# Attention with its backward pass: Q and dO turned by the crossbar, next head's loads gated, usual path last, last turns early

## The chip, the cores and the metric

One core of one Trainium2 chip. The metric is the device time of one execution in microseconds (us). Every comparison is with the kernel before, run on the same chip in the same rounds.

## The reference, cut to what matters

The forward function is a layer norm, attention of 32 heads (2048 queries, 2048 keys, head size 128, width 576), and a gated feed-forward block; the output is `x + s * g`. What is computed is the output and the gradients of nine arguments.

```python
def _A_ref(x, k_cache, v_cache, wq, wo):
    q = (x @ wq).reshape(B, Sq, H, Dh).transpose(0, 2, 1, 3)
    p = softmax(einsum("bhqd,bhkd->bhqk", q, k_cache) * Dh ** -0.5)
    o = einsum("bhqk,bhkd->bhqd", p, v_cache)
    return o.transpose(0, 2, 1, 3).reshape(B, Sq, H * Dh) @ wo
...
_out, _vjp = jax.vjp(_f, A_x, A_k_cache, A_v_cache, A_wq, A_wo, ...)
return (_out, *_vjp(grad_out))
```

## The kernel before

Attention takes 3053 of 4944 us. A head has two phases of 16 query tiles. In the first, TensorE makes the scores of a tile, ScalarE their exponentials (the tile Pq), and SyncE has the crossbar turn Pq into PT (128 x 2048, 0.52 MB), which TensorE needs six tiles later for `o`. In the second, dP is made, VectorE forms dS in the place of Pq, SyncE has it turned into dST, and TensorE needs that six tiles later for `dq`. The row sums' inverse `rinv` is not put into P but into dOn and Qn, the natural layouts of dO and Q, on VectorE. QT and KT, the turned Q and K, are two halves of one tile KQ, and the profile calls both KQ: `Qn<-KQ` is Q turned back, `KQ<-Kn` is K turned.

```python
def transpose_slab(hs, qt, name):            # PT and dST, 32 a head, all on SyncE
    T = wpt.tile([P, NT, P], bf, name=name, tag="PT")      # 8 buffers
    nc.sync.dma_start_transpose(T[:], hs.slabs[qt][:])
def turn_nat(dst, src): nc.sync.dma_start_transpose(...)   # VT, KT: one each a head
def prep_don(hs, sc): pe_transpose_blocks(... dOT -> dOn)  # TensorE, then a copy by VectorE
def prep_qn(hs):      pe_transpose_blocks(... QT -> Qn)    # TensorE, then a copy by VectorE
def scale_qn(hs, qt): nc.vector.tensor_scalar(Qn[:, qt], Qn[:, qt], rinv[:, qt], op0=mult)
def tail1(hs, qt, part):                     # o = P V, and junk = -(o . dOn), into negdelta
    tail_part(hs, hs.PT[qt], hs.Vn, part) ...
# ... the plan of a head: b1, b2 = first slot of its two phases, pl = second phase of the head before
for c in range(4):
    put(pl + q(c), 0, lambda c=c: load_k(hd(), c, 4))            # 4 pieces of 128 KB
    put(pl + q(skew + 3 + c), 0, lambda c=c: load_v(hd(), c, 4))
put(pl + q(4), 0, lambda: load_wo(hd()))
put(pl + q(5), 0, lambda: load_wq(hd()))
```

`put` names a slot of the program, but the scheduler that orders each engine's instructions moves them; a place is only sure if a dependency holds it. Loads and stores are issued by GpSimd, turns by SyncE, each strictly in order.

## Time and profile before

| | us |
|---|---|
| median of 3 runs (lowest to highest) | 4947.64 (4942.96 to 4948.25) |
| span of the profiled run | 4943.5 |
| attention, first score matmul to the first matmul after it | 3052.8 |
| one steady head (mean of 28 heads, from PT 0 to the next PT 0) | 95.0 |

### The profile page before, as it was taken

The page shows a single profiled execution, that of the slowest core. Times are in us where ns is not written, and L with a number is a line of the kernel's source. Part 1 is how long each engine was busy: PE and PEld are TensorE (multiplying, and loading weights), DVE is VectorE, ACT ScalarE, POOL GpSimd, SP SyncE. Part 2 cuts the span into 40 slices and gives each one's busy share as a digit, 9 for nine tenths or more (in the row PEclk, how much of TensorE's full clock was granted, in tenths as well). Part 3 has the DMA queues.
Part 4 walks back from the last instruction along what each step waited for, and adds up shares of the span by engine and source line. Part 5 has one row for each costly group of instructions (what it writes and reads, how often), then busy time and mean ns, then how long its engine had stood idle before and what let it go on. Part 6 is the DMA issues. An engine that isn't in the chain of part 4 may idle for free. (4 is left out here: it accounts for less than half of the span.)

```text
span 4943.5 us, 101621 instructions
## 1 busy us (share of the span) xinstructions
PE 4877.6 (99%) x41029; PEld 2892.8 (59%) x41029; DVE 2802.9 (57%) x6554; ACT 2473.9 (50%) x4228; POOL 843.4 (17%) x1329
## 2 busy tenths in 40 slices
PE   9999999999999999999999999999899999999998
PEld 4445666666666666666666666666455555555554
DVE  4544666666566666666656666666434555554225
ACT  4431766766676676676666667667312111111011
POOL 3322111111111111111111111111221111111111
PEclk9999999999999999999999999999999999999999
DMA  7887999999999999999999999999999999998665
GB/s 260 274 202 173 225 222 225 228 229 230 222 231 224 230 225 237 219 227 220 235 220 231 233 224 229 231 221 231 210 225 235 223 234 218 233 226 204 195 168 151
DMA packets 3048181, 1097.68 MB, mean 222 GB/s; under 512 B 2951890, under 2 KB 2956115, under 8 KB 3047699
## 3 DMA queue, kind: packets, MB, share of 16 engines
q1 hardware_dynamic: 2948930, 771.66, 83.4%
q0 software_dynamic: 98160, 318.85, 20.3%
q8 instruction: 322, 5.28, 0.4%
q14 instruction: 161, 1.31, 0.1%
q10 hardware_dynamic: 608, 0.59, 0.0%
HBM read 175.31 MB, written 177.93 MB: 71 GB/s over the span
## 5 line engine op out<-in xcount | busy, mean ns | idle before, releaser
L654 ACT ACTIVATE Pq<-sp 128x1024 bf16<-128x1024 f32 x1024 | 1048.0, 1024 | 268.7 <-PE sp L636 259.4
L709 DVE SCALAR_TENSOR_TENSOR Pq<-dp,negdelta,Pq 128x1024 bf16<-128x1024 f32 x512 | 655.2, 1280 | 44.5 <-PE dp L706 44.5
L712 ACT ACTIVATE t<-dp,negdelta 128x1024 bf16<-128x1024 f32 x512 | 567.6, 1115 | 214.3 <-PE dp L706 199.8
L636 PE MATMUL sp<-KQ 128*128 128x512 bf16 x2048 | 609.6, 379 | 2.2 <-ACT Pq L654 2.1
L706 PE MATMUL dp<-VT,dOT 128*128 128x512 bf16 x2048 | 609.2, 379 | 2.3
L683 PEld LDWEIGHTS <-dST 128*128 128x128 bf16 x8192 | 506.8, 98 | 155.5 <-DMA dST<-Pq 16.3
L683 PEld LDWEIGHTS <-PT 128*128 128x128 bf16 x8192 | 499.8, 98 | 133.6 <-DMA PT<-Pq 14.1
L683 PE MATMUL acc<-Kn,dST 128*128 128x128 bf16 x8192 | 556.3, 219 | 9.0 <-DMA dST<-Pq 8.8
L683 PE MATMUL acc<-Vn,PT 128*128 128x128 bf16 x8192 | 542.0, 219 | 8.6 <-DMA PT<-Pq 8.3
L713 DVE TENSOR_TENSOR Pq<-t,Pq 128x1024 bf16<-128x1024 bf16 x512 | 354.6, 693 | 319.3 <-ACT t L712 307.0
L744 PE MATMUL acc<-Pq,dOn 128*128 128x512 bf16 x2048 | 531.1, 379 | 0.0
L744 PE MATMUL acc<-Pq,Qn 128*128 128x512 bf16 x2048 | 526.7, 380 | 0.0
L724 ACT ACTIVATE dq_n<-acc,rsc 128x128 bf16<-128x128 f32 x512 | 187.7, 367 | 335.1 <-PE acc L683 313.6
L1154 DVE TENSOR_TENSOR dxn<-acc,dxn 128x576 f32<-128x576 f32 x272 | 206.1, 758 | 248.1 <-PE acc L1054 248.1
L744 PEld LDWEIGHTS <-Qn 128*128 128x128 bf16 x2048 | 200.4, 98 | 240.8 <-issue 1.5
L744 PEld LDWEIGHTS <-dOn 128*128 128x128 bf16 x2048 | 198.9, 98 | 233.8
L1116 ACT ACTIVATE ndh<-dh 128x512 bf16<-128x512 f32 x144 | 86.0, 597 | 452.5 <-DVE du_blk L1114 448.7
L641 DVE TENSOR_REDUCE rs_all<-rsp 128x1 f32<-128x2 f32 x512 | 78.4, 153 | 306.4 <-ACT Pq L654 294.8
L636 PEld LDWEIGHTS <-KQ 128*128 128x128 bf16 x2048 | 179.3, 98 | 124.4 <-issue 4.0
L706 PEld LDWEIGHTS <-dOT 128*128 128x128 bf16 x2048 | 178.7, 98 | 124.6 <-issue 12.4
L677 POOL DMA_DIRECT2D on_d<-o_n x128 | 97.4, 761 | 784.3 <-DVE junk L695 460.3
L677 POOL DMA_DIRECT2D dq_d<-dq_n x128 | 98.2, 768 | 721.4 <-ACT dq_n L724 681.7
(208 smaller groups left out, 6827.6 us busy)
## 6 DMA issues: line engine op xcount, KB each, us to landing
out_dram<-kvn POOLq DMA_DIRECT2D x64, 512.0 KB, 4.8
ah<-a_d POOLq DMA_DIRECT2D x18, 1024.0 KB, 9.3
ah<-h_d POOLq DMA_DIRECT2D x18, 1024.0 KB, 11.7
h_d<-h_row POOLq DMA_DIRECT2D x64, 256.0 KB, 3.5
a_d<-a_row POOLq DMA_DIRECT2D x64, 256.0 KB, 3.9
x_all<-in_A_k_cache_dram SPq DMA_DIRECT2D x64, 256.0 KB, 4.0
on_d<-o_n POOLq DMA_DIRECT2D x128, 128.0 KB, 4.6
kvT_d<-KQ POOLq DMA_DIRECT2D x32, 512.0 KB, 5.7
```

The source lines that it names most:

```text
L636: nc.tensor.matmul(sp[:, c * CH:(c + 1) * CH], lhsT=hs.QT[:, qt * P:(qt + 1) * P], rhs=hs.KT[:, hf * HW_ + c * CH: hf * HW_ + (c + 1) * CH ...
L654: nc.scalar.activation(Pq[:, hsl], sp[:], AF.Exp, scale=SCALE, accum_out=hs.rsp[:, hf:hf + 1])
L677: nc.gpsimd.dma_start(dst_d[q0 * P:(qt + 1) * P, hs.h * P:(hs.h + 1) * P].rearrange("(t p) d -> p t d", p=P), buf[:])
L683: nc.tensor.matmul(hs.acc[:, 0, :], lhsT=T[:, kt, :], rhs=rhs[:, kt, :], start=(kt == 0), stop=(kt == NT - 1))
L706: nc.tensor.matmul(dp[:, c * CH:(c + 1) * CH], lhsT=hs.dOT[:, qt * P:(qt + 1) * P], rhs=hs.VT[:, hf * HW_ + c * CH: hf * HW_ + (c + 1) * C ...
L709: nc.vector.scalar_tensor_tensor(Pq[:, hsl], dp[:], hs.negdelta[:, qt:qt + 1], Pq[:, hsl], op0=ALU.add, op1=ALU.mult)
L712: nc.scalar.activation(t[:], dp[:], AF.Identity, bias=hs.negdelta[:, qt:qt + 1], scale=1.0)
L713: nc.vector.tensor_tensor(Pq[:, hsl], t[:], Pq[:, hsl], op=ALU.mult)
L724: nc.scalar.activation(hs.dq_n[:, qt % G4, :], hs.acc[:, 0, :], AF.Copy, scale=hs.rsc[:, qt:qt + 1])
L744: nc.tensor.matmul(self.acc, lhsT=self.nat[:, qt, :], rhs=self.slabs[qt][:, cs], start=(qt == self.lo), stop=(qt == self.hi - 1))
L1116: nc.scalar.mul(ndh[:], dh[:], -1.0)
L1154: nc.vector.tensor_tensor(dxn[:, st, :], acc[:, :D], dxn[:, st, :], op=ALU.add)
```

## The change

The intent: take 1024 transposes from TensorE, the engine that is always busy, by turning dO and Q on the crossbar; load the next head's K, V, wq and wo in whole pieces at chosen times, away from the stores; make the unused path the one that is jumped to; and turn the last group's operands early.

```diff
+            def turn_T(dst, src, lo, hi):
+                nc.sync.dma_start_transpose(dst[:, lo:hi, :], src[:, lo * P:hi * P])
...
-                    for c in range(4):
-                        put(pl + q(c), 0, lambda c=c: load_k(hd(), c, 4))
-                        put(pl + q(skew + 3 + c), 0, lambda c=c: load_v(hd(), c, 4))
-                    put(pl + q(4), 0, lambda: load_wo(hd()))
-                    put(pl + q(5), 0, lambda: load_wq(hd()))
+                    def gated(slot, dst, fn):
+                        def run():
+                            nc.gpsimd.tensor_copy(dst(), heads[h - 1].slabs[slot % NT][0:1, 0:1])
+                            fn(hd())
+                        put(slot, 0, run)
+                    gated(pl + q(1), lambda: hd().Kn[0:1, 0, 0:1], load_k)
+                    gated(pl + q(5), lambda: wo_h[0:1, 0:1], lambda hs: (load_wo(hs), load_wq(hs)))
+                    gated(pl + q(skew + 6), lambda: hd().Vn[0:1, 0, 0:1], load_v)
...
-                    put(b1 + q(sc + 1), nb * P, lambda sc=sc: prep_don(hd(), sc))
+                NDON = 2 if NSC % 2 == 0 else 1
+                for c in range(NDON):
+                    put(b1 + q((c + 1) * NSC // NDON), 0, lambda c=c: turn_T(hd().dOn, hd().dOT, ...))
...
-                put(b1 + q(NTH + 2), NT * P, lambda: prep_qn(hd()))
+                put(b1 + q(NTH + 1), 0, lambda: turn_T(hd().Qn, hd().QT, 0, NT))
...
-    with tc.If(flag > 0) as branch:
+    with tc.If(flag < 1) as branch:
+        attention(False)
+    with branch.Else():
         attention(True)
-    with branch.Else():
-        attention(False)
...            (and, after attention, the last group's turns of wq and dqb issued earlier)
```

A gate is a copy of one element from a tile into the buffer that is to be loaded: the load must wait for it, and it for the tile.

More of the change, by code (lines that the diff above doesn't have):

```diff
@@ L806, in plan @@
                     put(b1 + q(sc), DT * CH, lambda sc=sc: prep_dot(hd(), sc))
-                    put(b1 + q(sc + 1), nb * P, lambda sc=sc: prep_don(hd(), sc))
+                NDON = 2 if NSC % 2 == 0 else 1
+                for c in range(NDON):
+                    put(b1 + q((c + 1) * NSC // NDON), 0, lambda c=c: turn_T(hd().dOn, hd().dOT, c * NT // NDON, (c + 1) * NT // NDON))
                 for qt in range(NT):
-                    put(b1 + max(qt + 1, q(2 + qt // nb)), 0, lambda qt=qt: scale_don(hd(), qt))
+                    put(b1 + max(qt + 1, q((qt * NDON // NT + 1) * NSC // NDON + 2)), 0, lambda qt=qt: scale_don(hd(), qt))
                 put(b1 + q(NTH + 3), 0, lambda: turn_nat(hd().VT, hd().Vn))
-                put(b1 + q(NTH + 2), NT * P, lambda: prep_qn(hd()))
+                put(b1 + q(NTH + 1), 0, lambda: turn_T(hd().Qn, hd().QT, 0, NT))
                 for qt in range(NT):
@@ L1173, with last_turns, dx_more @@
             wqT2 = blk.tile([P, HG, D], bf, name="wqT2")
-            def dx_more(st, both=False):
+            def last_turns():
+                nc.sync.dma_start_transpose(wqT2[:], A_wq[:, (NHG - 1) * HC:])
+                turn_rows(dqbT2, onqs[(NHG - 1) % 2][1], 0, NTE, HG)
+            def dx_more(st, both=False, w=wqT):
                 acc = ps.tile([P, WD], f32, name="acc")
-                terms = [(dqbT[:, st * HG + hl, :], wqT[:, hl, :]) for hl in range(HG)]
+                terms = [(dqbT[:, st * HG + hl, :], w[:, hl, :]) for hl in range(HG)]
                 if both:
@@ L1206 @@
             NQ = max(1, NT // 4)
+            if NHG == 2:
+                last_turns()
             for hg in range(NHG):
@@ L1212 @@
                 ends = list(range(NTE)) if early else list(range(NTE, NT)) if final else []
-                nc.sync.dma_start_transpose(wqT, A_wq[:, cols])
+                if not (final and NTE):
+                    nc.sync.dma_start_transpose(wqT, A_wq[:, cols])
                 def turn_dq(a, b):
@@ L1217 @@
                 turn_dq(NTE if final else 0, NTE if early else NT)
-                if early:
-                    nc.sync.dma_start_transpose(wqT2[:], A_wq[:, (hg + 1) * HC:(hg + 2) * HC])
-                    turn_rows(dqbT2, onqs[(hg + 1) % 2][1], 0, NTE, HG)
                 dwq = wp.tile([P, DT, HC], bf, name="dwq")
@@ L1233, in ends_rows @@
                                 st = todo_rows.pop(0)
-                                finish(st, dx_more(st, early))
+                                finish(st, dx_more(st, early, wqT2[:] if final and NTE else wqT))
                                 if st + 2 <= ends[-1]:
@@ L1261 @@
                         nc.vector.tensor_tensor(dxn[:, st, :], acc[:, :D], dxn[:, st, :], op=ALU.add)
+                if hg == NHG - 3:
+                    last_turns()
                 while todo_rows:
```

## The prediction

> **What bounds the kernel now.** I read the busy shares and the forty slices first, then the groups of instructions kept apart by shape, then TensorE alone in order of time in the middle of attention, then the stretches where its idle time lies.
>
> ```profile
> PE 4877.6 (99%) x41029; PEld 2892.8 (59%) x41029; DVE 2802.9 (57%) x6554; ACT 2473.9 (50%) x4228; POOL 843.4 (17%) x1329
> ...
> DMA  7887999999999999999999999999999999998665
> ```
>
> TensorE is busy all the time and no other compute engine is above 57%, but the DMA row is as full as TensorE's: two candidates for the bound. The Trainium skill warns that matmul busy time says little (page "Perfetto Trace Analysis", § Identifying the Most-Contended Engine), so I take the distance from one matmul's start to the next. In the middle of attention:
>
> ```profile
> 2003.70 0.39 PE L145 MATMUL acct<-ident,dOT 128*128 128x128 bf16 x4
> 2003.93 1.24 PE L215 MATMUL acc<-dsT,woT_h 128*128 128x512 bf16 x5
> ...
> 2030.12 1.06 PE L145 MATMUL acct<-ident,KQ 128*128 128x128 bf16 x16
> 2031.01 0.59 PE L636 MATMUL sp<-KQ 128*128 128x512 bf16 x2
> ```
>
> Sixteen transposes take 31.01 - 30.12 = 0.89 us of TensorE's time, 0.056 each; pairs of 512 columns are 0.43 apart, 0.216 a matmul. I summed, over all of attention (483 to 3535 us), the excess of each distance over these pitches: 50 us of 3053, so 98.4% of attention is matmuls back to back. TensorE is the bound, really. Of the 50 us, 21 lie before matmuls that wait for a crossbar transpose (PT, dST; 24 times, over half of it in the first and last head), 11 before dp, which waits for VectorE. The rest of the kernel loses 9 us before attention and 32 after it, nearly all in two places shown below.
>
> **How full are the DMA engines?**
>
> ```profile
> 1000.00:1500.00 500.00, 499.64 (x4440) 313.62 (x4439) 325.62 (x855) 338.01 (x573) 73.59 (x117) 1.00 1.15 228
> ```
>
> The first is a stretch of attention, its DMA share next to last; the second, the transposes with the median us from issue to landing.
>
> ```profile
> PT<-Pq SPq DMA_TRANSPOSE x512, 4.8
> dST<-Pq SPq DMA_TRANSPOSE x512, 5.2
> ```
>
> The share of 1.15 counts packets that overlap, so it can't be read as a limit. I binned the packet records of 600 to 3450 us by quarters of a microsecond: the transposing queue moves up to 291 GB/s while it runs, plain transfers about 460. Needed are 189 and 36 GB/s. 189/291 + 36/460 = 0.73: an estimate, from these records, that a quarter of the DMA time is free on average. A 128x2048 transpose (0.52 MB) then costs 1.8 us of the DMA engines.
>
> **What the Trainium skill says.** (1) "TensorE: Matmul & The Clock Gate", § Part 4: PE-mode transpose gives about 275 ns for a 128x128 transpose inside a kernel, into PSUM, with a copy after it. The trace's record is 219 ns, but the pitch is 56 ns; the pitch decides what removing one is worth. (2) "Advanced Engine Details and Errata", § X-Bar Transpose (TRN2) expects 350 to 400 GB/s for crossbar transposes, like plain DMAs; this trace shows 291 at best. (3) "Runtime: NRT & Kernel Launch", § Instruction fetch mechanics: a taken branch whose target is outside the two pages held forces a fetch before execution goes on. The trace agrees, at the end of attention, where the kernel jumps over the unused path:
>
> ```profile
> 3536.07 2.61 PE L958 MATMUL acc<-dsT,KQ 128*128 128x512 bf16 x20 [1.07 <-issue]
> 3542.99 2.81 PE L958 MATMUL acc<-dsT,KQ 128*128 128x512 bf16 x14 [4.31 <-issue]
> 3543.62 0.56 POOL L933 DMA_DIRECT2D dsg<-dsg_d  x1 [6.98 <-issue]
> ...
> 3547.92 0.76 POOL L575 DMA_DIRECT2D Kn<-in_A_wo_dram  x1 [0.32 <-issue]
> ...
> 3555.41 0.90 PE L958 MATMUL acc<-Kn,KQ 128*128 128x512 bf16 x6 [1.77 <-DMA Kn<-in_A_wo_dram]
> 3560.08 1.60 PE L958 MATMUL acc<-Vn,KQ 128*128 128x512 bf16 x6 [3.77 <-DMA Vn<-in_A_wo_dram]
> ```
>
> TensorE stalls 1.07 + 4.31 us for nothing but issue, GpSimd 6.98; then TensorE waits for weights that GpSimd asked for late, and after each stall runs for some us at half pitch. The stretch of 3535 to 3583 loses about 16 us.
>
> **The change part by part.**
>
> *Natural layouts by crossbar.* Per head 16 transposes of dOT and 16 of QT leave TensorE; the instruction order of the built kernel confirms 1024 fewer, with the other matmuls of a steady head in nearly the same order. At a pitch of 0.0555 us: 1024 x 0.0555 = 56.8 us, all on the path. VectorE loses the copies (54.4 + 41.1 us of busy time), off the path. Added per head: two transposes of 128x1024 and one of 128x2048, 1.05 MB, 3.6 us of DMA. Needed DMA time goes from 0.73 x 94.9 = 69.3 us a head to about 73 of 93.1: 78%, hidden on average.
>
> *Where they stand in the in-order queue of SyncE.* In the built order the Qn turn follows the PT of tile 5 and must wait until TensorE has done with the old Qn in tile 7; PT of tile 6 stands behind it, then the VT turn, then PT of tile 7 (before: PT 7, then VT). In the trace the VT turn started at 2029.94, when the store of the old VT had landed. PT 7 would then start after 2030.5, land some 5 us later at 2035 to 2036, and is wanted at about 2037. The slack there shrinks to 1 or 2 us. VectorE, also in order, will wait 1 to 2 us for dOn and Qn at their scaling in each head; it has slack and four accumulators stand between it and TensorE. I charge 4 us in all for these.
>
> *Gated loads.* The 512 KB load of K and those of wo move out of tiles 5 to 8, where they stood beside the stores and the transposes. Of the 21 us of transpose waits, 5 may go.
>
> *Usual path last.* The taken branch moves from the end of attention to its start. At the end some 7 us go: the stalls of 1.07 + 4.31 and the half pitch, while most of the waits for Kn and Vn stay, since those loads still start only after attention. At the start each engine now jumps: I charge 4 us, less than at the end, as TensorE waited 2.1 us there for ScalarE's table anyway. Net -3.
>
> *Early turns for the last group.*
>
> ```profile
> 4840.01 4.33 SPq L1049 DMA_TRANSPOSE dqbT<-dqb  x1
> ...
> 4846.52 1.16 PE L1054 MATMUL acc<-wqT,dqbT 128*128 128x512 bf16 x8 [3.80 <-DMA dqbT<-dqb]
> ...
> 4896.82 2.13 PE L1054 MATMUL acc<-wdT,dqbT 128*128 128x512 bf16 x16 [2.39 <-DMA dqbT<-dqb]
> ```
>
> The turn of the last group's dqb went to SyncE fourth in a row at 4840; now it goes before the others, when its load has landed (about 4831), and the last group needs no new wqT. The waits of 3.80 and 2.39 go, with some half pitch after the first (1.7): 8 us. TensorE sets the end here, so they count in full.
>
> Sum: -56.8 + 4 - 5 - 3 - 8 = -69 us; 4947.6 - 69 = 4879, rounded to 4878.
>
> **The rivals.** (a) *The DMA queue becomes the bound.* For it: DMA slices of 9 throughout, landings up to 12 us, PT 7 behind two turns that wait. Against it: a quarter of the DMA time is free, and a PT is wanted six tiles after it is made. If each head lost 1.5 us, 32 x 1.5 = 48 us would be given back: about 4926. (b) *ScalarE takes over in the first half of a head.* A tile of exponentials there costs 2 x (1.02 + 0.20) = 2.44 us, with a dq_n 2.81, and a tile of TensorE without transposes 2 x 0.43 + 0.89 + 0.86 = 2.6. Only tiles 4 and 5 are over, by 0.2 us each; 32 x 0.4 gives back 13 at most: about 4891. (c) *The gating also clears most of the waits*, and the branch costs nothing at the start: 4878 - 10 - 4 gives about 4862.
>
> **Range and chances.** The 56.8 us are counted work and sure unless (a) takes them; the rest is small. 8 times in 10 between 4860 and 4905. For over 2%, below about 4850, another 28 us would have to come from a kernel that loses 91 us in all, of which I have spent 16 already: chance 0.03. Slower by over 2% would need 3 us lost per head on top of the saving: 0.01. Within 2%: 0.96.
>
> **What would show it.** In the profile after: no TensorE transposes in attention and a steady head of 93.1 us instead of 94.9; transposes dOn<-dOT and Qn<-KQ on SyncE, landing in about 5 us; waits of matmuls for PT and dST still near 20 us in all; the 4.31 us stall gone from the end of attention and one of a few us at its start; no wait for dqbT in the last 110 us. I'm wrong if a head stays near 95 us with waits for PT around tiles 12 and 13 (a), or if the stall at the start, or the weights after attention, cost over 10 us.

## More of the kernel before

The lines that the prediction quotes are not repeated. Two groups that it did not quote are the measure for what follows: the two products that consume the turned tiles. The columns are: line, engine, operation, output and inputs, shapes, count; then busy us and mean ns; then the idle time of TensorE just before them and what ended most of it.

```profile
L683 PE MATMUL acc<-Kn,dST 128*128 128x128 bf16 x8192 | 556.3, 219 | 9.0 <-DMA dST<-Pq 8.8
L683 PE MATMUL acc<-Vn,PT 128*128 128x128 bf16 x8192 | 542.0, 219 | 8.6 <-DMA PT<-Pq 8.3
```

In 3 ms TensorE waits 17.6 us for turned tiles.

## The result, and the profile after

| | before | after |
|---|---|---|
| median of 4 runs, us (lowest to highest) | 4947.94 (4942.96 to 4948.41) | 5119.8 (5093.86 to 5144.63) |
| profiled span | 4943.5 | 5092.0 |
| attention in it | 3052.8 | 3210.7 |
| all the rest of it | 1890.7 | 1881.3 |

The ratio is 1.0349, 95% interval 1.0297 to 1.0401: slower. Ratios here are the mean time of one kernel's runs over that of the other's of the same rounds, so not quite the ratio of the medians. The profiled run is the fastest of the kernel after.

Attention grew by 158 us; all the rest (the span less attention) shrank by 9. So the branch and the early turns did their work, and attention lost. The page's busy line of the kernel after, and the two groups again:

```profile
PE 4846.2 (95%) x39250; PEld 2863.9 (56%) x40005; DVE 2693.5 (53%) x6362; ACT 2474.5 (49%) x4228; POOL 757.8 (15%) x1236
```

```profile
L686 PE MATMUL acc<-Kn,dST 128*128 128x128 bf16 x8192 | 557.6, 220 | 68.0 <-DMA dST<-Pq 61.0 <-DVE dOT L42 4.3 <-ACT part L48 0.7
L686 PE MATMUL acc<-Vn,PT 128*128 128x128 bf16 x8192 | 556.9, 222 | 103.3 <-DVE junk L698 94.1 <-DMA PT<-Pq 5.7
```

The idle time before the two products rose from 17.6 to 171.3 us, in two kinds: waits for VectorE (`junk`), and waits for dST. (The busy line can't be compared with that of before: some of TensorE's records are missing from this trace, 39250 matmuls against 40005 weight loads. The idle columns are safe from that.) The view of waits, with us in total, times and the longest:

```profile
DVE Qn L675 <- DMA Qn<-KQ: 200.6, 31, 11.8
DVE dOn L672 <- DMA dOn<-dOT: 134.0, 32, 7.4
PE acc L686 <- DVE junk L698: 94.1, 31, 8.4
```

VectorE waits once a head for Qn, and TensorE waits once a head for VectorE. One head in order of time, SyncE, then VectorE, then TensorE (start, us, engine, line, operation; in brackets the idle time before and what ended it):

```profile
2089.62 6.16 SPq L633 DMA_TRANSPOSE PT<-Pq  x2
2095.86 3.25 SPq L618 DMA_TRANSPOSE Qn<-KQ  x1
2099.21 1.63 SPq L633 DMA_TRANSPOSE PT<-Pq  x1
2101.02 2.01 SPq L615 DMA_TRANSPOSE VT<-Vn  x1
```

```profile
2100.45 1.23 DVE L675 TENSOR_SCALAR Qn<-Qn,rinv_all 128x128 bf16<-128x128 bf16 x7 [6.39 <-DMA Qn<-KQ]
```

```profile
2102.95 1.86 PE L686 MATMUL acc<-Vn,PT 128*128 128x128 bf16 x16 [2.94 <-DVE junk L698]
2104.60 1.06 PE L639 MATMUL sp<-KQ 128*128 128x512 bf16 x2
```

SyncE comes to Qn's turn only at 2095.86, because the tiles ahead of it are late; VectorE stands before its scaling for 6.39 us, and behind it in VectorE's order stand the `junk` products that free TensorE's accumulators. The stall costs more than its 2.94 us. The view of stretches has the granted clock third from the end, then the DMA share and GB/s:

```profile
2099.00:2103.00 4.00, 1.05 (x6) 0.42 (x5) 2.48 (x17) 1.97 (x4) 0.02 (x1) 0.98 1.03 226
2103.00:2107.00 4.00, 4.00 (x24) 2.53 (x24) 2.90 (x15) 1.11 (x2) 0.73 (x1) 0.59 1.11 211
```

After a stall of some 3 us the matmuls run at a granted clock of 0.59 for 4 us; that is another 1.6 us.

**How much room the turns had.** The landings can be followed through the trace. For each PT or dST I took the end of the exponential or of the product that made its source, and the end of SyncE's instruction that turned it. The difference is how late SyncE runs (its lag); and where the source was ready only after SyncE's instruction before had ended, the queue was idle in between. Means over 30 heads, worked out from the records of the traces:

| lag in us behind tile | 0 | 3 | 5 | 7 | 9 | 11 | 13 | 15 | queue idle, us a head |
|---|---|---|---|---|---|---|---|---|---|
| before, PT | 4.7 | 1.9 | 3.0 | 5.9 | 8.9 | 7.6 | 7.2 | 6.0 | 3.85, all before tiles 0 to 6 |
| before, dST | 5.1 | 5.2 | 7.9 | 7.9 | 10.5 | 8.6 | 7.1 | 5.5 | 0.05 |
| after, PT | 6.3 | 3.6 | 4.9 | 7.8 | 10.9 | 6.4 | 5.5 | 4.5 | 0.52 |
| after, dST | 4.3 | 6.3 | 6.2 | 6.5 | 14.5 | 13.1 | 11.5 | 7.4 | 0.58 |

In the kernel before, the transposing queue is idle for want of a tile 3.9 of 95 us, 4%, and nearly all of it early in the first phase. From tile 7 to the end of a head it is 0.05 us. The prediction had taken a quarter of the DMA time to be free.

The table counts waits for a tile's own source alone. In the kernel after, SyncE also stands before the K turn, 3.5 us a head against 0.2 before (gaps between its instructions), until the store of what stood in its place has landed:

```profile
SPq L615 <- DMA kvT_d<-KQ: 105.3, 29, 6.0
```

So its queue was not busy all the time. What that wait is worth is tested below (`g2_gatefull`, `c3_tie_gatefull`).

### The profile page after: what moved, and what is told of

Its sections match the earlier page's. It is cut to its first block, busy times and chain, and to the rows that moved or that the text cites. A ratio compares the mean times of both kernels' runs of the same rounds, so it can differ in the third digit from the quotient of the medians.

```text
span 5092.0 us, 98687 instructions
## 1 busy us (share of the span) xinstructions
PE 4846.2 (95%) x39250; PEld 2863.9 (56%) x40005; DVE 2693.5 (53%) x6362; ACT 2474.5 (49%) x4228; POOL 757.8 (15%) x1236
## 5 line engine op out<-in xcount | busy, mean ns | idle before, releaser
L686 PE MATMUL acc<-Vn,PT 128*128 128x128 bf16 x8192 | 556.9, 222 | 103.3 <-DVE junk L698 94.1
L686 PEld LDWEIGHTS <-PT 128*128 128x128 bf16 x8192 | 513.2, 99 | 231.9 <-issue 106.7
L639 PE MATMUL sp<-KQ 128*128 128x512 bf16 x1890 | 589.9, 388 | 6.2 <-issue 2.4
L709 PE MATMUL dp<-VT,dOT 128*128 128x512 bf16 x1919 | 586.0, 382 | 2.1
L747 PE MATMUL acc<-Pq,Qn 128*128 128x512 bf16 x1983 | 511.6, 379 | 6.7
L675 DVE TENSOR_SCALAR Qn<-Qn,rinv_all 128x128 bf16<-128x128 bf16 x512 | 115.7, 259 | 200.7 <-DMA Qn<-KQ 200.6
```

Of the source, the lines that this page charges most:

```text
L639: nc.tensor.matmul(sp[:, c * CH:(c + 1) * CH], lhsT=hs.QT[:, qt * P:(qt + 1) * P], rhs=hs.KT[:, hf * HW_ + c * CH: hf * HW_ + (c + 1) * CH ...
L686: nc.tensor.matmul(hs.acc[:, 0, :], lhsT=T[:, kt, :], rhs=rhs[:, kt, :], start=(kt == 0), stop=(kt == NT - 1))
L709: nc.tensor.matmul(dp[:, c * CH:(c + 1) * CH], lhsT=hs.dOT[:, qt * P:(qt + 1) * P], rhs=hs.VT[:, hf * HW_ + c * CH: hf * HW_ + (c + 1) * C ...
L747: nc.tensor.matmul(self.acc, lhsT=self.nat[:, qt, :], rhs=self.slabs[qt][:, cs], start=(qt == self.lo), stop=(qt == self.hi - 1))
```

## The experiments

Eighteen kernels ran, each in 3 rounds beside the kernel before (medians 4944.8 to 4951.1). First the four parts alone, then mends of the waits seen, then tests of what the queue can take. Where a group line is shown, it is one of the same pair as above (the line number shifts with the edit). Two theories stood against each other from the start: two in-order queues that make each other wait, and a queue that is full (at first called DMA capacity).

### The parts alone

`p1_qn`: only Q by the crossbar.

```diff
-                put(b1 + q(NTH + 2), NT * P, lambda: prep_qn(hd()))
+                put(b1 + q(NTH + 1), 0, lambda: turn_T(hd().Qn, hd().QT, 0, NT))
```

> The kernel before with Q's natural layout alone by crossbar. Theory of the in-order waits: VectorE stands some 6 us a head at the first scaling of Qn, TensorE about 3 us a head for an accumulator and some more at the half clock after it; with 28 us saved in transposes: slower, 5010 to 5070 us. Rival, DMA capacity: dO by crossbar moves as many bytes, so this run and the run of dO alone lose alike, each about +80 us (5030).

Measured: 5071.0 us, ratio 1.0242 (1.0223 to 1.0261), at the upper edge of the in-order theory. The wait for VectorE is all here (the waits for dST are 5.6 us):

```profile
L686 PE MATMUL acc<-Vn,PT 128*128 128x128 bf16 x8192 | 558.2, 222 | 118.0 <-DVE junk L698 110.4 <-DMA PT<-Pq 7.3
```

`p2_don`: only dO by the crossbar (its lines of the diff above).

> The kernel before with dO's natural layout alone by crossbar. In-order waits: VectorE waits about 4 us a head for dOn, but early in the head where it has slack, so most of the 28 us of 512 transposes is gained: 4915 to 4940 us. Rival, DMA capacity: slower by as much as Q alone, about 5030 us.

Measured: 4970.2 us, 1.0048 (1.0031 to 1.0066), a miss: waits for PT rose to 33 us, and VectorE waited 117 us for dOn. The two halves stand behind PT 1 and PT 3, just where the queue had its idle time; that fell from 3.9 to 0.1 us a head. It used all the idle time there was and was not free for that: 24 us lost and 28 us of TensorE's work taken away (512 transposes at 0.0555) make a price of 52 us. That it lost less than Q alone spoke against the full queue at this point; `p1_qn` has the wait for `junk` on top.

`p3_gate`: only the gated loads.

> The kernel before with the gated loads alone. In-order waits: the second, ungated part of the wo load blocks GpSimd some 10 us a head until woT has been turned, the store of KQ behind it is late, SyncE waits for that store ahead of KQ's turn, and dST behind it comes late: TensorE waits for dST over 40 us more in all, 4990 to 5040 us. Rival, DMA capacity or the crossbar turns alone at fault: the gating moves no byte and costs nothing or gains, 4935 to 4950 us.

Measured: 5017.4 us, 1.0133 (1.0116 to 1.0151), as the in-order theory said. The waits that it named are in the trace: GpSimd stood 279.0 us before the second part of wo (30 times, until woT had been turned), and SyncE 105.1 us before the K turn.

```profile
L683 PE MATMUL acc<-Kn,dST 128*128 128x128 bf16 x8192 | 566.2, 221 | 66.2 <-DMA dST<-Pq 64.1
L683 PE MATMUL acc<-Vn,PT 128*128 128x128 bf16 x8192 | 541.9, 219 | 2.5 <-DMA PT<-Pq 0.6
```

The waits for PT went, as meant, and the waits for dST grew by seven times as much. By the order of issues in the traces, K was loaded beside PT 4 to 6 before and beside dST 0 now, wo beside PT 4 and 5 and now dST 2 to 7, V beside dST 2 to 4 and now dST 7 to 9; wo's own turn went from the first phase to behind dST 5. The lag behind PT 9 fell from 8.9 to 6.9 us, behind dST 9 it rose from 10.5 to 14.3.

`p4_ends`: only the branch and the early last turns.

> The kernel before with the swapped branch and the earlier turns of the last group alone. The trace of the changed kernel shows the stretch after attention 11.5 us shorter and the start of attention 2.2 us later: 4936 to 4942 us. Rival: the swap costs more at the start than it saves: 4948 us or more.

Measured: 4936.0 us, 0.9976 (0.9959 to 0.9992), as expected; these two parts are called the ends below. It is the best of all versions and beats both kernels.

The four ratios give +120, +24, +66 and -12 us, +198 in all, against +173 for the whole: the loss is in the parts, and partly shared.

### Mending the waits that were seen

`c1_tie`: the kernel after, with the scaling of Qn made to depend on the row sum of tile 12, so that VectorE meets it later.

```diff
+                nc.vector.tensor_copy(hs.rq[:], hs.rinv_all[:, :QTIE])      # QTIE = 13
-                nc.vector.tensor_scalar(hs.Qn[:, qt, :], hs.Qn[:, qt, :], hs.rinv_all[:, qt:qt + 1], ...)
+                nc.vector.tensor_scalar(hs.Qn[:, qt, :], hs.Qn[:, qt, :], hs.rq[:, qt:qt + 1], ...)
```

> The changed kernel, but with the scaling of Qn for tiles 0 to 12 tied to the row sum of tile 12 (a copy of the reciprocals, made there, is what they read), so that VectorE meets the first wait for the Qn turn some four tiles later; SyncE's order is the same. If VectorE standing at Qn ahead of the accumulators' evictions is the first cause: TensorE's waits behind junk (99 us) and the half clock after them go, 4970 to 5010 us. Rival, the extra turn holds up SyncE and the DMA engines, and VectorE's wait only shows it: 5080 us or more.

Measured: 5137.6 us, 1.0397 (1.0372 to 1.0422), a clear miss. The wait for `junk` is gone, and its time came back as waits for the turns:

```profile
L693 PE MATMUL acc<-Kn,dST 128*128 128x128 bf16 x8192 | 566.8, 222 | 130.4 <-DMA dST<-Pq 125.1 <-DVE dOT L42 3.6
L693 PE MATMUL acc<-Vn,PT 128*128 128x128 bf16 x8192 | 550.4, 221 | 75.8 <-DMA PT<-Pq 70.8 <-DVE o_n L50 0.9 <-DVE part L42 0.3
```

So VectorE's wait was not the only cause of the loss in the whole version; another one of the same size stood behind it.

`g2_gatefull`: only the gated loads, with the gate written to all parts of wo and to wq, since the second part of wo had slipped past the gate and blocked GpSimd (13.4 us at most).

```diff
-gated(pl + q(5), lambda: wo_h[0:1, 0:1], ...)
+gated(pl + q(5), lambda: [wo_h[0:1, 0:1], wo_h[0:1, DT * P - 1:DT * P], hd().wq[0:1, 0, 0:1]], ...)
```

> The kernel before with the gated loads as in the run of the gating alone, but the gate also writes into what the second part of the wo load and the wq load fill, so that these can't be hoisted ahead in GpSimd's queue. If the hoisted second part of wo is what cost 66 us: 4935 to 4955 us. Rival, the new times of the loads themselves crowd dST: 4990 us or more.

Measured: 5002.0 us, 1.0117 (1.0076 to 1.0159), a miss: the blocking of GpSimd was worth little (1.0133 before this mend), though SyncE no longer stood before the K turn. Most of the waits for dST stayed (54.1 us), and at 19 of these 32, with 43 of the 54 us, the same things stood in the 15 us before: the K turn (`KQ<-Kn`, behind dST 7), and V's load of 0.5 MB beside the dST after it. SyncE, then GpSimd, then TensorE:

```profile
2388.59 1.92 SPq L615 DMA_TRANSPOSE KQ<-Kn  x1
2390.61 11.15 SPq L630 DMA_TRANSPOSE dST<-Pq  x3
```

```profile
2390.94 0.54 POOL L177 DMA_DIRECT2D Vn<-in_A_v_cache_dram  x1 [0.39 <-PE acc L215]
```

```profile
2400.39 1.89 PE L683 MATMUL acc<-Kn,dST 128*128 128x128 bf16 x16 [4.84 <-DMA dST<-Pq]
```

Three turns took 11.15 us there, 3.7 each, where 2.8 is the mean of dST in this run.

`c3_tie_gatefull`: both mends in the kernel after.

> The changed kernel with both mends. In-order waits: both losses go, 5120 - 130 - 66: 4900 to 4945 us. Rival, DMA capacity: both crossbar turns still there, 5000 us or more.

Measured: 5114.2 us, 1.0335 (1.0317 to 1.0353), a miss: as slow as the kernel after, although neither the wait for `junk` nor SyncE's before the K turn is left. The two products now stand 117.7 (dST) and 78.9 us (PT), nearly all of it for turned tiles.

`c4_ends_qn_tie`: the branch and last turns, and Q by the crossbar with the tied scaling; loads and dO as before.

> The kernel before with the swapped branch, the earlier last turns, and Q alone by crossbar with the tied scaling; loads and dO as before. In-order waits: 4936 less most of 28 us, 4905 to 4930 us. Rival, DMA capacity: above 4950 us.

Measured: 4976.3 us, 1.0053 (1.0031 to 1.0075), a miss. `p1_qn` and the ends together would be 1.0242 - 0.0024 = 1.0218; the tie took 0.0165 of that away, 82 us. But it is still 38 us slower than the ends alone (1.0053 against 0.9976), with 28 us less work on TensorE (512 transposes at 0.0555):

```profile
L693 PE MATMUL acc<-Kn,dST 128*128 128x128 bf16 x8192 | 556.4, 219 | 16.8 <-DMA dST<-Pq 14.5
L693 PE MATMUL acc<-Vn,PT 128*128 128x128 bf16 x8192 | 543.9, 219 | 62.3 <-DMA PT<-Pq 58.4 <-DVE Qn L676 1.4 <-DVE rinv_all L645 1.0
```

### Is it the place of the turn?

The Qn turn stands two places ahead of the V turn, and I took it to wait there for the old Qn. (The traces do not show that wait: SyncE's gap before the Qn turn is over 0.15 us in 1 of 30 heads of the kernel after and in none of `c4_ends_qn_tie`.) The theory of the next four was that moving things apart would do. All but `g3_vlate` contain the ends.

`q3_late`: as `c4_ends_qn_tie`, the turn in two halves held behind PT 12 and 14 by one-element writes, the scaling put into the second phase but not tied.

```diff
+                def held(at, dst, fn):
+                    def run():
+                        nc.vector.tensor_copy(dst(), hd().rinv_all[0:1, at:at + 1])
+                        fn()
+                    put(b1 + at, 0, run)
+                for c, at in ((0, 12), (1, 14)):
+                    held(at, lambda c=c: hd().Qn[0:1, c * NTH, 0:1], lambda c=c: turn_T(hd().Qn, hd().QT, c * NTH, (c + 1) * NTH))
```

> The kernel before with the branch and the early last turns, and with Q turned by the crossbar, but the turn in two halves that stand behind PT 12 and PT 14 in SyncE's queue (held there by a one-element write that needs that tile's row sum), and all scaling of Qn in the second phase. Same number of turns and bytes as the earlier run with only the scaling tied, where the turn stood behind PT 5 and two places ahead of the V turn. Theory 'order' (the turn costs because it stands in an in-order queue next to the V turn and waits there for the old Qn): the PT waits of TensorE fall from 46-78 us to under 20, no junk wait, and the kernel takes 4890 to 4915. Theory 'full queue' (the transposing instructions fill 92% of the attention stage before, 94 to 96% with the added turns, so any added 2 us per head has nowhere to go): it stays within 10 us of 4976, or at best 4950.

Measured: 5162.1 us, 1.0438 (1.0421 to 1.0455), worse than all. The scheduler had moved VectorE's scaling forward again, to right behind tile 13's row sum, and SyncE came to the turn some 8 us late:

```profile
DVE Qn L675 <- DMA Qn<-KQ: 241.6, 55, 11.4
```

The test says nothing on the place of the turn, but how dear a wait in VectorE's order is. SyncE in turn was ahead of its work: idle for want of a tile 16 us a head.

`d3_late`: the same idea for dO. Its result is wrong: tile 0 was scaled after its first use. The times stand.

```diff
+                put(b1 + 2, 0, lambda: turn_T(hd().dOn, hd().dOT, 0, NTH))
+                put(b1 + 8, 0, second_half)      # held by a one-element write of rinv of tile 8
+                    put(b1 + max(qt + 1, 6 if qt < NTH else 12), 0, lambda qt=qt: scale_don(hd(), qt))
```

> The same with dO in place of Q: the first half of dOn turned behind PT 1, the second held behind PT 9, the scaling of the first half at tiles 6 to 8 and of the second from tile 12, so that VectorE should not reach a half before it has landed. Theory 'order': VectorE's dOn wait of 117 us falls under 20, PT waits under 20, and the kernel takes 4905 to 4930 (4936 with the ends alone, less the 28 us of TensorE transposes, plus what remains). Theory 'full queue': 4940 to 4960 as in the run with dO alone less the ends' 15 us (4955).

Measured: 5056.9 us, 1.0226 (1.0208 to 1.0243): VectorE waited 265 us for dOn.

`g3_vlate`: as `g2_gatefull`, V's gate at the last tile of the second phase instead of tile 12.

```diff
-gated(pl + q(skew + 6), lambda: [hd().Vn[0:1, 0, 0:1]], load_v)
+gated(pl + q(NT - 1), lambda: [hd().Vn[0:1, 0, 0:1]], load_v)
```

> The kernel before with only the loads gated in full as in the earlier run (5002 us), but V held to the last tile of the second phase in place of tile 12. In the earlier run nearly every wait of TensorE for dST has the KQ turn (tile 11) and the V load beside the next dST (5 to 7 us long) within 15 us before it. Theory 'meeting' (the two stand together): the dST waits fall from 48-65 us to under 20 and the kernel takes 4940 to 4960. Theory 'any 512 KB load in one piece beside a dST costs': the waits stay about 40 us or more, the kernel stays over 4980.

Measured: 4970.1 us, 1.0056 (1.0028 to 1.0085), between the two ranges. Taking V away from the K turn gave back 30 of the 58 us (1.0117 to 1.0056), and the waits for dST fell to a third:

```profile
L683 PE MATMUL acc<-Kn,dST 128*128 128x128 bf16 x8192 | 558.7, 220 | 19.6 <-DMA dST<-Pq 19.5
L683 PE MATMUL acc<-Vn,PT 128*128 128x128 bf16 x8192 | 541.9, 219 | 3.3 <-DMA PT<-Pq 3.1 <-issue 0.2
```

That is half of the loss (the two intervals still overlap a little). V's load now also stands beside dST 11 to 14, where the lag is smaller, so the meeting with the K turn is not shown to be the reason. It is still not better than the loads as they were.

`a3_all`: all three of these together, with the branch and last turns (wrong result, as `d3_late`).

> All parts with the three placements mended: Q and dO by the crossbar at the held places, loads gated in full with V last, branch and last turns. Theory 'order and meeting': 4865 to 4900, the first version with all parts that beats the kernel before. Theory 'full queue': 5000 or more, with TensorE waiting for PT and dST for over 100 us, since both added turns are there and nothing is left of the slack.

Measured: 5123.8 us, 1.0358 (1.034 to 1.0377), with VectorE waiting 285 us for dOn and 186 for Qn. TensorE's waits for PT and dST are only 5 us: the time fits the theory of the full queue, but not for its reason, and nothing is learned on it here.

### Is the queue full?

`x1_vt2`: the kernel before, V turned a second time into the same place from the same data. Nothing is waited for, and nobody soon waits for it.

```diff
                 put(b1 + q(NTH + 3), 0, lambda: turn_nat(hd().VT, hd().Vn))
+                put(b1 + q(NTH + 3), 0, lambda: turn_nat(hd().VT, hd().Vn))
```

> The kernel before with one thing added: V is turned a second time behind PT 9, into the same buffer from the same data, so the result is the same. It costs the transposing queue some 2.1 us per head where its lag is longest (9 us in the kernel before), but it waits for nothing and nobody soon waits for it. Theory 'full queue': the added 67 us of transposes have nowhere to go; PT waits of 40 us or more, plus 30 to 60 us (4980 to 5010). Theory 'two in-order queues': the lag rises by 2 us, which the six tiles between turn and use can hold: at most plus 15 us (4945 to 4962).

Measured: 5007.9 us (4977.5 to 5018.5), 1.0108 (1.0070 to 1.0146). In the profiled run (5014.3 us, near the median) attention is 68 us longer and the two groups read:

```profile
L683 PE MATMUL acc<-Kn,dST 128*128 128x128 bf16 x8192 | 557.6, 219 | 33.4 <-DMA dST<-Pq 33.1
L683 PE MATMUL acc<-Vn,PT 128*128 128x128 bf16 x8192 | 543.2, 219 | 36.9 <-DMA PT<-Pq 35.8 <-DVE rs_all L641 0.4 <-DVE part L42 0.3
```

One turn more per head cost 53 us by the ratio and 68 in this run's attention. It brought no new wait: SyncE stands 0.5 us a head before the two V turns together, as before the one. 32 turns at 2.1 us each (the guess beforehand) or at 2.9 (the mean V turn in this run) would be 67 or 92 us if none of it were hidden. That is the theory of the full queue, and far from the 15 us at most of the other. The idle time in it fell from 3.9 to 1.8 us a head all the same; the added turn spread beyond its own 2.9 us, as the mean PT turn rose from 2.43 to 2.53.

`q5_tied`: as `q3_late`, the scaling tied to the last tile's `negdelta`, so that neither in-order wait is left.

```diff
+                nc.vector.scalar_tensor_tensor(hs.rq[:], hs.negdelta[:], 0.0, hs.rinv_all[:], op0=ALU.mult, op1=ALU.add)
```

> As the run with Qn's turn in two halves behind PT 12 and PT 14 (5162 us, where TensorE's PT and dST waits were almost gone, but VectorE met Qn at once and waited 242 us for it), now with the scaling of Qn tied to the last tile's negdelta, so that VectorE meets it only about five tiles into the second phase. Theory 'two in-order queues' (the loss is what SyncE's lag, 8 to 9 us at those tiles, makes VectorE wait, nothing else): VectorE's wait for Qn under 15 us, PT and dST waits under 20 us, and 4880 to 4905, faster than both kernels. Theory 'full queue': 4950 or more, the waits for PT and dST back at 46 us or more as in the run with the turn beside the V turn (4976).

Measured: 4989.4 us, 1.0081 (1.0058 to 1.0103). VectorE's wait is gone, and TensorE stands 46.7 + 36.8 us before the two products:

```profile
L690 PE MATMUL acc<-Kn,dST 128*128 128x128 bf16 x8192 | 559.4, 220 | 46.7 <-DMA dST<-Pq 45.7
L690 PE MATMUL acc<-Vn,PT 128*128 128x128 bf16 x8192 | 545.1, 220 | 36.8 <-DMA PT<-Pq 35.1 <-DVE dOn L672 0.6 <-DVE rinv_all L645 0.5
```

A better place for the Qn turn does not help: 28 us of TensorE's work were removed, and 66 us of waits put in (83.5 against 17.6).

`d5_tied`: the ends, and dO's turns with the scaling tied to the row sums of tiles 5 and 13, in the right order.

```diff
+                nc.vector.tensor_copy(hs.rd[:, lo:lo + 6], hs.rinv_all[:, lo:lo + 6])   # lo = 0, 8
```

> As the run with dO's second half turned behind PT 9 (5057 us, 265 us of VectorE waits for dOn, and a wrong result because tile 0 was scaled after its use), now scaled in the right order and tied to the row sums of tiles 5 and 13, just before the first use. Theory 'two in-order queues': VectorE's dOn wait under 40 us, 4905 to 4930. But the room is small: dOT is ready at tile 1 or 2 and dOn needed at tile 6, and SyncE lags 2 to 5 us there; if the wait stays over 60 us, 4945 to 4970. Theory 'full queue': 4955 as with the dO turns in their old places less the ends.

Measured: 4973.6 us, 1.0055 (1.0034 to 1.0076): correct, and no better than `p2_don` less the ends (1.0048 - 0.0024 = 1.0024). VectorE still waited 102 us for dOn: it is made from dOT at tile 1 or 2 and needed at tile 6, and SyncE is late by up to 4 us.

`a5_ends_q_d`: the ends, `q5_tied` and `d5_tied` together, loads as before.

> Branch, last turns, and both crossbar parts as in the two runs above, loads as in the kernel before. Theory 'two in-order queues': the sum of the two, 4855 to 4890. Theory 'full queue': both turns together take the queue past what it can do; over 4980, with PT and dST waits over 60 us.

Measured: 5056.1 us, 1.0219 (1.0181 to 1.0257), idle time before the two products 138.8 us. More turns, more loss: against the ends alone (0.9976) dO's halves cost 39 us, Q's 52, and both 120.

`s6_swap`: `q5_tied` with V turned on TensorE again, so both engines have as much to turn as before.

```diff
-                put(b1 + q(NTH + 3), 0, lambda: turn_nat(hd().VT, hd().Vn))
+                put(b1 + q(NTH + 3), NT * P, lambda: prep_vt(hd()))
```

> The run with Qn's turn held late and its scaling tied (4989 us), with one thing changed: V is turned on TensorE again (16 transposes a head at a pitch of 0.056 us, copied out by VectorE), so the transposing queue has as many turns as in the kernel before and TensorE as many transposes. Theory 'full queue' (what counts is the amount of turning, not whose turn it is): the waits for PT and dST fall from 82 us back to under 30, and it takes 4925 to 4950, like the run with the branch and the last turns alone (4936). Theory 'the Qn turn is dear in itself, wherever it stands': over 4965.

Measured: 4953.5 us (4940.3 to 4957.7), 1.0008 (0.9988 to 1.0028): 36 us less in the medians than `q5_tied`, and just above the range that I gave.

```profile
L690 PE MATMUL acc<-Kn,dST 128*128 128x128 bf16 x8192 | 557.9, 219 | 15.2 <-DMA dST<-Pq 13.0
L690 PE MATMUL acc<-Vn,PT 128*128 128x128 bf16 x8192 | 542.1, 219 | 6.0 <-DMA PT<-Pq 3.6 <-DVE dOn L672 0.6
```

The waits are back to 21 us (15.2 with the ends alone). So most of what Q's turn costs is the amount of turning, not that it is Q. The run contains the ends and has as many turns and transposes as they do alone, yet it is still 16 us slower (1.0008 against 0.9976); in the profiled runs 6 us of that are these waits, 7 are new ones of TensorE for VectorE before dP, and the rest was not followed.

`x3_load`: the kernel before, with 0.52 MB a head of plain loads more, in four gated pieces, into a tile that nobody reads.

```diff
+                    scr = hstat.tile([P, 4, P], bf, name="scr", bufs=1)
+                    nc.gpsimd.tensor_copy(scr[0:1, 0, 0:1], hd().slabs[at - 1][0:1, 0:1])      # at = 7, 9, 11, 13
+                    nc.gpsimd.dma_start(scr[:], A_v_cache[0, h].rearrange("(p t) d -> p t d", t=NT)[:, 4 * c:4 * c + 4, :])
```

> The kernel before with one thing added: 0.52 MB more of plain loads per head, as many bytes as one turn, in four pieces held to tiles 6, 8, 10 and 12 of the first phase, into a scratch tile that nobody reads. If the transposing queue is full because its packets and the plain ones share the DMA engines, a plain load takes its place in the queue's time: plus 20 to 45 us, waits for PT up from 8.6 to 25 us or more. If it is full because of its own issuing and order on SyncE alone: under plus 8 us.

Measured: 4997.6 us (4977.3 to 5010.1), 1.0111 (1.0092 to 1.0130). The loss is above the 20 to 45 us that I gave, the wait for PT (20.9 us) under the 25. The profiled run is the fastest of the four, so its waits may be the least:

```profile
L683 PE MATMUL acc<-Kn,dST 128*128 128x128 bf16 x8192 | 557.0, 219 | 13.9 <-DMA dST<-Pq 12.0
L683 PE MATMUL acc<-Vn,PT 128*128 128x128 bf16 x8192 | 542.9, 219 | 23.6 <-DMA PT<-Pq 20.9 <-DVE rs_all L641 0.4
```

A plain load, issued by another engine, costs about as much as a turn of as many bytes. The trace shows that the turns themselves got longer: the mean PT turn is 2.58 us (2.43 before), while dST, beside which nothing was added, stayed at 2.57 (2.59). Among PT 8 to 15 in this run, the turns that ran beside one of these loads took 2.57 us (114 of them), the others 2.25 (126). So it is not SyncE's issuing alone that is full; the turns lose time to transfers that another engine issued, which fits what the two kinds share, the DMA engines. (The gates also hold GpSimd: it stood 303.6 us until the piece before had landed. What part of the 55 us that is was not told apart.)

The view of stretches, for 600 to 3400 us, shows the same from another side. The last number is GB/s; the first fence is the kernel before, the second the one after (`x1_vt2` has 228 GB/s, `x3_load` 231).

```profile
600.00:3400.00 2800.00, 2791.20 (x24797) 1750.18 (x24795) 1796.64 (x4781) 1901.60 (x3243) 404.95 (x642) 1.00 1.16 227
```

```profile
600.00:3400.00 2800.00, 2637.06 (x22142) 1633.48 (x22559) 1599.80 (x4323) 1800.86 (x3072) 311.15 (x530) 0.98 1.16 226
```

The kernel after moves 1.05 MB a head more. Had that been hidden, the rate would have risen by 1.05 MB / 95 us = 11 GB/s; it is the same. 1.05 MB at 226 GB/s are 4.6 us, x 32 = 149 us, near the 158 us by which attention grew. That agreement is a check, not a proof: the kernel after loses part of its time to VectorE's waits, and `p2_don` did reach 232 GB/s by using the idle time.

## Why the prediction was wrong

- **Natural layouts, -56.8 us on the path.** The count was right (1024 transposes fewer), and no run speaks against the pitch; `s6_swap` against `q5_tied` shows that 512 transposes on TensorE are the cheaper side by 36 us. But the saving counts in full only as long as TensorE alone sets the pace.
- **DMA: "0.73 x 94.9 = 69.3 us a head to about 73 of 93.1: 78%, hidden on average".** This step failed first. It divided the bytes by the best rates that each kind of transfer reaches (291 and 460 GB/s) and added the shares, as if both held throughout and did not disturb each other. In 1 us bins of the same records (600 to 3400 us) the transposing queue moved 220 GB/s on average where no plain transfer ran, and 139 where plain ones moved 50 to 150 GB/s. All together reach 227, and the lag shows the queue idle 4% of the time, not 27%. One turn of 0.52 MB a head, priced at 1.8 us and hidden, cost 53 us in all, 1.7 a head, in the open (`x1_vt2`). The rival (a), "the DMA queue becomes the bound", was the right one; it was sized at 1.5 us a head, and the head grew from 95.0 to 100.2 us instead of shrinking to 93.1, so 7 us a head were given back.
- **In-order queues, "I charge 4 us in all for these".** VectorE's wait is 6.5 us a head for Qn and 4.2 for dOn, not 1 to 2; the "slack and four accumulators" did not hold it, and TensorE stood behind `junk` for 94 us. I had taken Qn's turn to start when its source was free, not when SyncE, 8 us late, came to it. Taking this wait away gave back 82 of `p1_qn`'s 120 us (`c4_ends_qn_tie`); in the whole version it hid a wait of the queue of the same size, as `c1_tie` shows.
- **PT 7's slack of "1 or 2 us"** was right in kind: around the two turns, PT waits of 58 us came as soon as VectorE no longer waited (`c4_ends_qn_tie`). In the kernel after there were only 5.7 us of them. The order was read wrongly by one place: in the trace Qn's turn stands behind PT 6, then PT 7, then V's turn, which did not move.
- **Gated loads, -5 us.** Wrong in sign: +66 alone. The waits for PT did go (8.6 to 2.5 us), but the loads of K and wo went from PT 4 to 6, where the queue had some idle time, to dST 0 to 7, where it has next to none, and V's to the place of the K turn.
- **Branch -3, last turns -8.** Right: `p4_ends` gave -12, and the rest of the kernel after is 9 us shorter. The waits for the weights after attention stayed near 6 us. The half pitch after stalls, of which the prediction speaks, is in the trace of the kernel before: a granted clock of 0.60 at 3543 to 3547 us and of 0.50 at 3560 to 3565.
- **Rivals (b), ScalarE, and (c), gating clears the waits**: nothing in the runs speaks for (b); (c) is refuted by `p3_gate`. (The sum, -68.8 us, gives 4879; 4878 is a slip of 1 us.)

What stays open: why one more turn costs most of its time when the queue still shows 1.8 us of idle a head; how much of `x3_load` is GpSimd being held; and the 16 us of `s6_swap`. All experiments used this kernel's eight tile buffers and six tiles of distance; that more of either would hide the turns is a rival that was not tested.

## What to carry to other kernels

Before moving work from a full engine to the DMA queue, measure that queue's idle time from the ends of its instructions and of those that make its sources; here the peak rate over a short stretch promised 27% of room, and there were 4%. Where this queue was full, 0.52 MB more a head cost 53 us as a turn and 55 as a plain load, and a load could be made dearer or cheaper by the tiles beside which it stood (1.0117 and 1.0056 for V's). A turn that an in-order engine will use must be ready before that engine comes to it, and the scheduler, not the place in the program, decides when that is.

## What the Trainium skill lacked or had wrong

- "Advanced Engine Details and Errata", § X-Bar Transpose (TRN2) expects 350 to 400 GB/s. With the queue idle only 4% of the time, transposes and plain transfers together reached 227 GB/s here in attention, and 232 in the kernel that used up that idle time (`p2_don`); a turn of 0.52 MB took 2.44 (PT) and 2.60 us (dST) on average.
- "Perfetto Trace Analysis", § Identifying the Most-Contended Engine tells to judge DMA by the use of HBM, and then to find which DMA resource binds. The first says little where most bytes go from one on-chip buffer to another: the page of the kernel before has 71 GB/s of HBM traffic against 222 GB/s moved in all, with the queue nearly full. What showed that here were the lag behind the source and the idle time before it (10.5 us, and 3.9 us a head); the section does not have this measure.
- "DMA: Bandwidth & Descriptors", § Issuing engines are not separate DMA queues says that transfers of different engines interleave on the same DMA engines. The longer turns of `x3_load` agree, and the section puts no price on it: 0.52 MB a head of plain loads from GpSimd cost 55 us beside SyncE's transposes, one turn a head of the same size 53.
- "TensorE: Matmul & The Clock Gate", § Part 4: PE-mode transpose gives 275 ns in a kernel. What a transpose costs the path here is its pitch of 56 ns; the crossbar took 2.44 us for 16, 153 ns each. With the queue full, TensorE was the cheaper place (`s6_swap`, 36 us).
